# The second-last output block of a conv + maxout-FFN kernel: stored by SyncE in two halves instead of by GpSimd as a whole

## The chip, the core and the metric

The kernel runs on one core of one Trainium2 chip. The metric is the device time of one execution in microseconds (us). The profile of one execution is read beside it: its span runs from the first to the last instruction that the profiler recorded on the core, and the execution's own time is a little longer than that span.

Five engines matter, each with its own instruction stream: TensorE (PE), VectorE (DVE), ScalarE (ACT), GpSimd (POOL) and SyncE (SP). SP only issues DMAs and waits. DMAs are issued here from SP, ACT and POOL, and show in the profile as queue q1 (SP), q10 (ACT) and q0 (POOL).

## The reference

```python
# attention stage: softmax over 7 taps per head, then a causal 7-tap convolution along the sequence
w = exp(weight - max); w = w / (sum(w) + 1e-09)              # weight: 8 heads x 7 taps
x_pad = zeros(6 rows) + x                                    # x: 8 x 4160 x 192
out[b, s, h*24+g] = sum_k w[h, k] * x_pad[b, s + k, h*24+g]
# FFN stage on the 33280 tokens of 192
h = maximum(maximum(x @ w1, x @ w2), x @ w3)                 # 192 -> 768
y = h @ w_out                                                # 768 -> 192, float32
```

The output is 33280 rows of 192 float32 numbers, 768 bytes a row.

## The kernel before, in words

The tokens are cut into 65 blocks of 512 (`NBLK`). Blocks 0 to 63 are eight blocks from each of the eight sequences. Block 64 gathers the last 64 rows (`HALF`) of each sequence. The order of all instructions is written out by hand (`tc.manual_schedule()`), so what stands first in the text is issued first on its engine.

The main loop runs `t` from 1 to 64. Each turn does the following.

- It computes the first FFN layer of block `t` in six pieces `l1(t, j)`, j from 0 to 5: TensorE fills two PSUM tiles, `lp` and `lq` (L383), ScalarE makes `r` from `lp` (L387), VectorE makes `h` from `r` and `lq` (L388).
- Between these pieces it computes the second layer of the block before, `st2(t - 1, j, NJ)`, also in six pieces. TensorE accumulates into PSUM tiles `po` (L426). When two of a block's four 128-token slices are ready, ScalarE copies one partial sum to `a` (L435) and VectorE adds the other and writes the output tile `o` (L436). This happens at j = 3 for the first two slices and at j = 5 for the last two.
- It convolves a later block (`conv`), repacks it by DMA (`repack`, L366, half on SP and half on POOL; `double`, L372, on SP) and loads x for a later block (`load_x`, L130, on SP). These stop as the loop runs out of blocks.
- At the end of the turn, `store(t - 1, 0, 4, (nc.gpsimd,))` issues one DMA on POOL that writes the whole 512 x 192 tile `o` of block `t - 1` (L452).

After the loop, `st2(64, u, 6)` finishes block 64. Its four slices end one by one, and after each pair there are two stores of 64 partitions x 2 slices x 192: for slices 0 and 1 both on SP, for slices 2 and 3 one on SP and one on ACT. So the kernel ends with five stores: block 63 from POOL (393 KB) and block 64 from SP, SP, SP and ACT (98 KB each).

```python
if t == NB - 1 and s % 2 == 1:
    store(t, s - 1, s + 1, (nc.sync, nc.sync if s == 1 else nc.scalar))
```

Behind the last of these instructions stands the closing code of the program, which the profile shows under L542. SP waits for every DMA counter of the program, a few counters to each instruction. Every engine runs a DRAIN and reports to POOL. POOL, after a DRAIN of its own, waits for the four reports and then releases the others. A second round of the same kind follows.

Of the kernel before, what the change touches and what calls it, by code (L numbers as in the profile page):

```python
# [27 lines left out]
def kernel(  # L28
# [12 lines left out]
    nc = tc.nc  # L41
# [27 lines left out]
    NB = len(blocks)  # L69
# [41 lines left out]
    def load_x(t):  # L111
        if not 0 <= t < NB:
            return
        chunks = chunks_of[t]
        n = len(chunks)
        xf = (xfp.tile([P, NQ, D], FP32, tag="xf", name=f"xf_{t}") if n <= NQ else
              const.tile([P, n, D], FP32, name=f"xf_{t}"))
        parts = []
        i, n = 0, len(chunks)
        row = [c[1] * SEQ + c[2] for c in chunks]  # L120
        while i < n:
            k = i
            while (k + 1 < n and chunks[k + 1][3] == chunks[i][3]
                   and row[k + 1] - row[k] == row[i + 1] - row[i]):
                k += 1
            step = row[i + 1] - row[i] if k > i else 0
            rlen = chunks[i][3]
            src = bass.AP(tensor=x.tensor, offset=row[i] * D,
                          ap=[[D, rlen], [step * D, k - i + 1], [1, D]])
            nc.sync.dma_start(out=xf[0:rlen, i:k + 1, :], in_=src)  # L130
            if parts and parts[-1][0] == rlen:
                parts[-1] = (rlen, parts[-1][1], k + 1)
            else:
                parts.append((rlen, i, k + 1))
            i = k + 1
        xin[t] = [xf, None, parts]

    def cast_x(t):
        if not 0 <= t < NB:
            return  # L140
        xf, _, parts = xin[t]
        n = len(chunks_of[t])
        x16 = x16s[t % 4] if n <= NQ else x16z
        v = x16[:, EDGE:EDGE + n * D].rearrange("p (q d) -> p q d", d=D)
        for (rl, q0, q1) in parts:
            nc.gpsimd.tensor_copy(out=v[0:rl, q0:q1, :], in_=xf[0:rl, q0:q1, :])  # L146
        xin[t][1] = x16
# [164 lines left out]
    def conv(t, pools=((psw, "w"), (psw, "w"))):  # L312
        if t >= NB:
            return
        G = [pool.tile([P, NBLK], FP32, tag=tag, name=f"G{i}_{t}") for i, (pool, tag) in enumerate(pools)]
        x16 = xin[t][1]
        for (q, b, row_lo, rlen, lo, hi, cc) in chunks_of[t]:
            for i in range(2):
                for g in range(4):
                    h = SLOTS[i][g]  # L320
                    cb = q * D + GRP * h + EDGE * (g % 2)
                    nc.tensor.matmul(  # L322
                        G[i][32 * g:32 * g + 32, lo:hi],
                        lhsT=x16[0:rlen, cb:cb + 32],
                        rhs=band[0:rlen, h, cc:cc + hi - lo],
                        start=True, stop=True, tile_position=(0, 32 * g))
        slots[t] = ysp.tile([P, 2, NBLK], FP16, tag="ys", name=f"ys_{t}")
        convs[t] = G
        xin.pop(t)
# [20 lines left out]
    def evac(t, i, copy=nc.scalar.copy):  # L350
        if t >= NB:
            return
        copy(out=slots[t][:, i, :], in_=convs[t][i][:])  # L353
# [5 lines left out]
    def repack(t):  # L359


        if t >= NB:
            return
        yd = dense[t] = ydp.tile([P, NC, NBLK], FP16, tag="yd", name=f"yd_{t}")
        for n, (half, s0, c, r0, rows) in enumerate(pieces):
            (nc.sync, nc.gpsimd)[n % 2].dma_start(out=yd[r0:r0 + rows, c, :],  # L366
                                                  in_=slots[t][s0:s0 + rows, half, :])

    def double(t):

        if NDENSE <= t < NB:
            nc.sync.dma_start(out=dense[t][HALF:P, :, :], in_=dense[t][0:HALF, :, :])  # L372

    def l1(t, j):


        N, y = blkN[t], dense[t]
        ps = [pool.tile([P, NBLK], FP32, tag=tag, name=f"l{tag}_{t}_{j}")
              for pool, tag in ((psp, "p"), (psq, "q"))]
        for c in range(NC):  # L380
            for i in range(2):
                row = slice(HALF * i, HALF * (i + 1))
                nc.tensor.matmul(ps[i][:, 0:N], lhsT=wd[row, c, P * j:P * (j + 1)],  # L383
                                 rhs=y[row, c, 0:N],
                                 start=(c == 0), stop=(c == NC - 1))
        r = rp.tile([P, NBLK], FP16, tag="r", name=f"r_{t}_{j}")
        nc.scalar.activation(out=r[:, 0:N], in_=ps[0][:, 0:N], func=AF.Relu)  # L387
        nc.vector.tensor_max(out=hs[t][:, j, 0:N], in0=r[:, 0:N], in1=ps[1][:, 0:N])  # L388
# [52 lines left out]
    def store(t, s0, s1, qs):  # L441
        if t < 0:
            return
        ob, segs = outs[t], blocks[t]
        if len(segs) == 1:
            r = segs[0][0] * SEQ + segs[0][1] + P * s0
            todo = [(0, P, r, P)]
        else:
            assert all((b, S, n, off) == (b, SEQ - HALF, HALF, HALF * b) for b, S, n, off in segs)
            todo = [(HALF * i, HALF, (2 * s0 + i) * SEQ + SEQ - HALF, 2 * SEQ) for i in range(2)]  # L450
        for i, (p0, n, r, step) in enumerate(todo):
            qs[i].dma_start(out=bass.AP(tensor=out.tensor, offset=r * D,  # L452
                                        ap=[[D, n], [step * D, s1 - s0], [1, D]]),
                            in_=ob[p0:p0 + n, s0:s1, :])

    assert all(n == NBLK for n in blkN)
    def begin(t):
        hs[t] = hp.tile([P, NJ, NBLK], FP16, tag="h", name=f"h_{t}")
        outs[t] = outp.tile([P, 4, D], FP32, tag="o", name=f"o_{t}")
# [33 lines left out]
    for t in range(1, NB):  # L493
        u = t + AHEAD
        load_x(t + 7)
        cast_x(t + 5)
        double(u - 1)
        begin(t)
        l1(t, 0)
        if t == 1:  # L500
            conv(u)
            evac(u, 0)
            evac(u, 1)
        elif t % 2 == 0:
            conv(u)
            conv(u + 1, ((psp, "p"), (psq, "q")))
            evac(u, 0)
            evac(u + 1, 0)
            evac(u + 1, 1, nc.vector.tensor_copy)
            evac(u, 1, nc.vector.tensor_copy)  # L510
        repack(u)
        st2(t - 1, 0, NJ)
        for j in range(1, NJ):
            l1(t, j)
            st2(t - 1, j, NJ)
        store(t - 1, 0, 4, (nc.gpsimd,))
    for u in range(NJ):
        st2(NB - 1, u, NJ)
# [28 lines left out]
```

The softmax here doesn't subtract the row's maximum and nothing guards it: scores larger than these inputs give would overflow.

## Time and profile before

| | |
|---|---|
| median of 5 runs | 482.11 us (481.77 to 484.03) |
| the profiled execution's own time | 481.93 us |
| its span | 479.9 us |
| mean granted TensorE clock | 0.995 |
| TensorE (PE) busy | 467.7 us, 97% of the span |
| VectorE, ScalarE, GpSimd busy | 365.9, 327.1, 211.2 us |
| last matmul group of the timeline starts | 473.04 us |
| last compute instruction (VectorE, tile `o`) | 474.08 to 474.43 us |

The profiled execution's time is 2.0 us longer than its span. Times in the views are counted from the start of the span. Register, branch, semaphore and DMA-issuing instructions are not counted as busy, and the chain of waits follows computing engines, so the closing code shows only when its line is asked for. A "q" behind an engine's name (SPq, POOLq) marks its sequencer.

### The profile page before, as it was taken

The numbers are of one execution on the slowest core, as the hardware profiler recorded it, in microseconds if no ns is written. First come the engines' busy times: TensorE is split into PE (matmuls) and PEld (weight loads), VectorE is DVE, ScalarE is ACT, GpSimd is POOL, SyncE is SP. The second block draws the span as 40 slices with busy tenths as digits, with TensorE's granted clock in tenths as the row PEclk, the third lists the DMA queues.
The fourth block names the chain that finished last, engine by engine and source line by source line (L and its number), as shares of the span: only waits on it lengthen the run. The fifth ranks groups of instructions, "written<-read, shape, count | busy, mean of one in ns | idle before, by whom it ended". The sixth has DMA issues, their size and how long they took to land.

```text
span 479.9 us, 21944 instructions
## 1 busy us (share of the span) xinstructions
PE 467.7 (97%) x9083; PEld 393.9 (82%) x9083; DVE 365.9 (76%) x609; ACT 327.1 (68%) x608; POOL 211.2 (44%) x341
## 2 busy tenths in 40 slices
PE   7899999999999999999999999999999999999994
PEld 3578888888888888888888888888888888888994
DVE  6667778777777878777787777778777777778774
ACT  5676676676667667676766766676676767667663
POOL 2654543554354355435435543543545354345210
PEclk9899999999999999999999999999999999999999
DMA  8877747665666666566566566665556666544312
GB/s 194 223 192 210 217 137 201 180 180 159 194 183 182 172 184 172 168 175 190 164 178 191 157 166 193 169 190 172 163 170 182 193 172 177 163 137 135 113 44 95
DMA packets 67603, 82.08 MB, mean 171 GB/s; under 512 B 9424, under 2 KB 55760, under 8 KB 67504
## 3 DMA queue, kind: packets, MB, share of 16 engines
q1 hardware_dynamic: 53934, 49.01, 40.0%
q0 software_dynamic: 13216, 31.38, 18.6%
q8 instruction: 71, 1.16, 1.1%
q10 hardware_dynamic: 354, 0.30, 0.2%
q14 instruction: 28, 0.23, 0.2%
HBM read 30.31 MB, written 25.56 MB: 116 GB/s over the span
## 4 chain that ended last, share of the span: by engine, by line
PE 97%; DVE 1%; ACT 1%; issue 0%; POOL 0%; POOLq 0%
PE lp L383 32%; PE po L426 30%; PE lq L383 26%; PE G L322 7%; PE D L342 1%; PE idle L196 1%; ACT band L268 0%; PE band_sum L245 0%; ACT r L387 0%; DVE xz L216 0%; DVE h L388 0%; PE pm L305 0%; PE wps L223 0%; PE pm L301 0%; DVE band L218 0%
## 5 line engine op out<-in xcount | busy, mean ns | idle before, releaser
L388 DVE TENSOR_TENSOR h<-r,lq 128x512 f16<-128x512 f16 x390 | 267.0, 685 | 101.8 <-ACT r L387 101.8
L387 ACT ACTIVATE r<-lp 128x512 f16<-128x512 f32 x390 | 232.8, 597 | 135.2 <-PE lp L383 89.8
L383 PE MATMUL lp<-yd,wd 64*128 64x512 f16 x1170 | 315.0, 376 | 0.1
L383 PE MATMUL lq<-yd,wd 64*128 64x512 f16 x1170 | 314.4, 375 | 0.0
L426 PE MATMUL po<-wo,h 64*128 64x192 f16 x3120 | 231.4, 243 | 0.5 <-issue 0.5
L426 PEld LDWEIGHTS <-h 64*128 64x128 f16 x3120 | 187.0, 94 | 26.4 <-issue 0.7
L383 PEld LDWEIGHTS <-wd 64*128 64x128 f16 x2340 | 164.6, 93 | 20.4 <-issue 0.7
L452 POOL DMA_DIRECT2D out_dram<-o x64 | 50.7, 792 | 246.0 <-DVE o L436 234.0
L366 POOL DMA_DIRECT2D yd<-ys x189 | 95.5, 509 | 2.3 <-ACT ys L353 1.6
L426 PE MATMUL po<-m,yd 64*128 64x192 f16 x780 | 87.0, 243 | 0.0
L436 DVE TENSOR_TENSOR o<-a,po 128x384 f32<-128x384 f32 (+1 forms) x132 | 71.4, 541 | 0.6 <-ACT a L435 0.6
L146 POOL CAST x<-xf 112x960 f16<-112x960 f32 x62 | 61.6, 995 | 2.9 <-DMA xf<-in_x_dram 1.7
L435 ACT COPY a<-po 128x384 f32<-128x384 f32 (+1 forms) x132 | 61.8, 469 | 1.2 <-PE po L426 1.2
L426 PEld LDWEIGHTS <-yd 64*128 64x128 f16 x780 | 55.1, 94 | 8.1
L322 PEld LDWEIGHTS <-x 112*32 112x32 f16 x2480 | 29.7, 96 | 13.3 <-issue 13.2
L353 DVE CAST ys<-G 128x512 f16<-128x512 f32 x60 | 38.5, 682 | 0.1
L353 ACT CAST ys<-G 128x512 f16<-128x512 f32 x66 | 35.8, 589 | 2.0 <-PE G L322 0.7
L322 PE MATMUL G<-band,x 112*32 112x103 f16 (+1 forms) x2480 | 34.7, 209 | 0.0
L161 POOL CAST xz<-xf 112x240 f16<-112x240 f32 (+2 forms) x6 | 2.4, 448 | 10.5 <-DMA xf<-in_x_dram 10.5
L196 PE MATMUL idle<-idle 128*128 128x512 f16 x14 | 5.6, 539 | 1.2 <-DVE unit L212 1.2
L342 PE MATMUL D<-band,xz 112*32 112x103 f16 (+1 forms) x240 | 4.3, 249 | 1.1 <-ACT band L268 1.1
L342 PEld LDWEIGHTS <-xz 112*32 112x32 f16 x240 | 4.0, 120 | 1.6 <-issue 1.5
(50 smaller groups left out, 40.9 us busy)
## 6 DMA issues: line engine op xcount, KB each, us to landing
out_dram<-o POOLq DMA_DIRECT2D x64, 384.0 KB, 4.1
xf<-in_x_dram SPq DMA_DIRECT2D x57, 420.0 KB, 4.6
yd<-yd SPq DMA_DIRECT2D x63, 192.0 KB, 3.3
yd<-ys SPq DMA_DIRECT2D x63, 48.0 KB, 3.7
yd<-ys POOLq DMA_DIRECT2D x63, 48.0 KB, 3.3
xf<-in_x_dram SPq DMA_DIRECT2D x8, 252.0 KB, 3.0
yd<-ys SPq DMA_DIRECT2D x63, 32.0 KB, 3.3
yd<-ys POOLq DMA_DIRECT2D x63, 32.0 KB, 3.1
```

What stands on the lines that cost most here:

```text
L146: nc.gpsimd.tensor_copy(out=v[0:rl, q0:q1, :], in_=xf[0:rl, q0:q1, :])
L322: nc.tensor.matmul(G[i][32 * g:32 * g + 32, lo:hi], lhsT=x16[0:rlen, cb:cb + 32], rhs=band[0:rlen, h, cc:cc + hi - lo], start=True, stop=T ...
L342: nc.tensor.matmul(ps[32 * g:32 * g + 32, lo:hi], lhsT=xz[t][0:rlen, q, v, 32 * s:32 * s + 32], rhs=band[0:rlen, h, cc:cc + hi - lo], star ...
L353: copy(out=slots[t][:, i, :], in_=convs[t][i][:])
L366: (nc.sync, nc.gpsimd)[n % 2].dma_start(out=yd[r0:r0 + rows, c, :], in_=slots[t][s0:s0 + rows, half, :])
L383: nc.tensor.matmul(ps[i][:, 0:N], lhsT=wd[row, c, P * j:P * (j + 1)], rhs=y[row, c, 0:N], start=(c == 0), stop=(c == NC - 1))
L387: nc.scalar.activation(out=r[:, 0:N], in_=ps[0][:, 0:N], func=AF.Relu)
L388: nc.vector.tensor_max(out=hs[t][:, j, 0:N], in0=r[:, 0:N], in1=ps[1][:, 0:N])
L426: nc.tensor.matmul(ps[b0, i][:, s % 2, :], lhsT=a, rhs=b, start=first, stop=last)
L435: nc.scalar.copy(out=a[:, ss, :], in_=ps[s0, 0][:, ss, :])
L436: nc.vector.tensor_add(out=outs[t][:, s0:s + 1, :], in0=a[:, ss, :], in1=ps[s0, 1][:, ss, :])
L452: qs[i].dma_start(out=bass.AP(tensor=out.tensor, offset=r * D, ap=[[D, n], [step * D, s1 - s0], [1, D]]), in_=ob[p0:p0 + n, s0:s1, :])
```

## The change

The loop's last turn (t = 64) no longer stores block 63 from POOL as a whole. Directly after j = 3, when slices 0 and 1 of block 63 have been added up, SP is given a store of these two slices (128 partitions x 2 x 192, 196 KB). At the end of the turn SP is given the store of slices 2 and 3. All other blocks are stored as before.

```diff
         for j in range(1, NJ):
             l1(t, j)
             st2(t - 1, j, NJ)
-        store(t - 1, 0, 4, (nc.gpsimd,))
+            if t == NB - 1 and j == 3:
+                store(t - 1, 0, 2, (nc.sync,))
+        if t == NB - 1:
+            store(t - 1, 2, 4, (nc.sync,))
+        else:
+            store(t - 1, 0, 4, (nc.gpsimd,))
     for u in range(NJ):
         st2(NB - 1, u, NJ)
```

In the built program SP's stream ends with five stores in place of three: block 63's two halves, then block 64's three. POOL's stream ends with the store of block 62. The streams of TensorE, VectorE and ScalarE are the same.

## The prediction

> **What bounds the kernel now.** I read the page first, then the chain of waits, then the timeline of the last 10 us, and last the closing code's line, L542, engine by engine. The chain is TensorE nearly everywhere, and it stops early:
>
> ```profile
> PE 97%; DVE 1%; ACT 1%; issue 0%; POOL 0%; POOLq 0%
> ```
>
> ```profile
> 473.75 0.32 ACT a L435
> 474.06 0.02 issue
> 474.08 0.35 DVE o L436
> ```
>
> The last computing instruction ends at 474.43, the span at 479.9. So 5.5 us pass after it, with stores and closing code only. The change touches nothing else: on TensorE, VectorE and ScalarE the instruction streams are the same, and up to 469 us the program is unchanged. What must be known is which wait ends last in these 5.5 us. The timeline gives the stores (columns: start, length, engine):
>
> ```profile
> 471.98 0.55 DVE L436 TENSOR_TENSOR o<-a,po 128x384 f32<-128x384 f32 x1
> ...
> 472.76 0.62 DVE L436 TENSOR_TENSOR o<-a,po 128x192 f32<-128x192 f32 x2 [0.23 <-ACT a L435]
> ...
> 472.83 0.75 POOL L452 DMA_DIRECT2D out_dram<-o  x1 [5.61 <-DVE o L436]
> ...
> 473.41 2.06 SPq L452 DMA_DIRECT2D out_dram<-o  x3
> ...
> 474.47 0.65 ACTq L452 DMA_DIRECT2D out_dram<-o  x1
> ```
>
> Then the closing code, SP's (475.5 to 478) and POOL's (up to 479.15), and for comparison POOL's first drain of the program, under L531:
>
> ```profile
> L542 SPq EVENT_SEMAPHORE  x9: 17/28/28, 475.5 to 477.8; - x9
> L542 SPq DRAIN  x2: 7/7/7, 477.8 to 477.9; - x2
> ```
>
> ```profile
> L542 POOLq DRAIN  x1: 6327/6327/6327, 472.8 to 472.8; - x1
> ```
>
> ```profile
> L531 POOLq DRAIN  x1: 183/183/183, 0.3 to 0.3; - x1
> ```
>
> SP has seen the last store land and has reported at 477.91 (the record's own start, 477.908, plus 7 ns). POOL's drain, which starts as its last store is issued, lasts 6.327 us and ends at 472.805 + 6.327 = 479.13. POOL's next instruction, the wait for the four reports, starts at 479.18 and waits for nothing; from there to the end of the span are 0.735 us. So the end is set by POOL's drain, and SP has 1.26 us to spare. The drains of POOL with no DMA before them took 0.18 us (above), 0.10 and 0.04 us (the two at 479.3 and 479.6). The long one is the only one that follows a POOL store, so I put its length down to that store.
>
> The Trainium skill, "Perfetto Trace Analysis", section "Sequencer-only Instruction (DRAIN, etc)", says that the profiled stretch of such an instruction begins when its waits are met, so that the 6.3 us would be work or flushing on POOL itself, not a wait for another engine. The record alone does not show that.
>
> **The change, part by part.**
>
> POOL's store goes. POOL's last DMA becomes block 62's, issued at 466.47. Its drain then starts at about 466.45. With the same 6.33 us it ends at 472.8, over 5 us before SP reports; if it is as short as the other drains, sooner still. Either way SP's report is what ends last. Its start 477.908 + 0.007, plus 0.044 us from the last report to POOL's next instruction (at the program's start POOL's drain ends at 0.496 and the next record starts at 0.540), gives 477.96 in place of 479.18: **1.22 us less**, if SP reports as early as before.
>
> SP's closing list gets shorter behind the last landing. SP checks the DMA counters in a fixed order, one instruction about 0.06 us after the other (nine records end the list: eight from 477.355 to 477.784, then the drain). Before, the last store's counter was the first in the list, so all the others came after the landing, seven waits. In the changed program the stores take the counters in turn, and the last one has the third: five waits are left behind it. 2 x 0.06 = **0.12 us less**.
>
> The first half moves to SP at j = 3. It waits for the VectorE add of 468.80 to 469.35. SP has nothing between 451.6 and 473.4, so nobody queues behind that wait but its own later stores. Issue costs 0.6 to 0.7 us (the three stores on SP: 596, 627 and 694 ns), landing 2.4 to 2.6 us after the start, all before 472.2. The engines move nothing then. Cost: nothing; the empty stretch of 4 us hides it.
>
> The second half on SP waits for the add that ends at 472.53 and is issued at about 472.57. At 0.69 us it leaves SP free at 473.31 with the 0.05 us gap that its issues have. Block 64's first store needs the add of 473.38 and started at 473.41. So **nothing is delayed as long as this issue takes at most 0.79 us**. Behind it stand all three SP stores of block 64, and the closing list waits for them. SP's issues of this kernel:
>
> ```profile
> L366 SPq DMA_DIRECT2D yd<-ys x189: 513/588/2417, 22.5 to 447.7; - x189
> L130 SPq DMA_DIRECT2D xf<-in_x_dram x73: 317/584/3772, 0.7 to 416.8; - x73
> ```
>
> The medians (588 and 584 ns, the second with up to 560 rows of 768 bytes against the half's 256) say that the length does not follow the number of rows; the long ones stand mostly where much other traffic runs. I take 0.65 us, zero delay; the far end is 2.42 us, a delay of 1.63 us, to be kept for the rivals.
>
> The transfers at the end change shape:
>
> ```profile
> q1 hardware_dynamic: 432, 0.30, 37.0%
> q0 software_dynamic: 69, 0.20, 18.9%
> q10 hardware_dynamic: 144, 0.10, 13.7%
> ```
>
> (474.6 to 477.3: queue, packets, MB, share.) Before, POOL's 393 KB ran alone from 474.16 to 475.10 at about 430 GB/s. Block 64's first row started only at 475.11, although its issue had ended at 474.11; where nothing is in the way, rows of an SP issue start 0.65 us after its end (the 2 x 112 load at 0.74: 0.648; the doublings, median 0.666), which is 474.76. So POOL's store held block 64 back by 0.35 us. From 475.11 on, 576 packets took 1.88 us; the third SP store, issued until 475.48 and able to start at 476.13, still had ScalarE's rows beside it and posted its last packet at 476.99. One store alone needs 0.5 us (144 packets, first to last of the first one: 475.11 to 475.62). After: the second half's rows start at 472.57 + 0.65 + 0.65 = 473.87, and 272 packets at the pace of 144 in 0.5 us take 0.95 us, until 474.82. The first store of block 64 starts there in place of 475.11, 0.3 us earlier, and the others follow in line; the third cannot start before 476.13 and not end before 476.63. So the last landing is **0.2 to 0.36 us earlier; I take 0.25**. If the half's own first row comes as late as block 64's did (1.70 us after the issue started), it ends at 475.2 and nothing is won: lower bound zero, or 0.1 us lost.
>
> Sum: 1.22 + 0.12 + 0.25 = 1.59 us. The profiled execution (481.93, span 479.9) would take 480.3; the median of the runs lies 0.2 us above it, so the forecast is 482.11 - 1.6 = **480.5 us**. The parts' ends give a gain of 1.24 (all certain parts, 0.1 lost in the transfers) to 1.70 us, 480.4 to 480.9.
>
> A rule of the skill speaks against this: "DMA: Bandwidth & Descriptors", section "Rules for kernel authors", with "Issuing engines are not separate DMA queues", says that all issuers share the same 16 DMA engines, that spreading DMAs over them saves only issue time, and that one large transfer beats two. By it the change would be worth nothing, since SP pays one issue more than POOL saves: 482.1. The row of the drain speaks otherwise, because it prices POOL as issuer and not the transfer.
>
> **The rivals.**
>
> *POOL's drain ends with the traffic, not with its own store.* There is one long drain in the trace, so a tie to the last landing cannot be excluded: it ended 1.78 us after 477.355. For it: the store itself had landed 2.9 us after its issue, at 475.7, so the drain outlived it by 3.4 us, which I cannot explain. Against it: the drain carries no wait. Then only the transfers' 0 to 0.36 us are won: 481.75 to 482.2. Chance 0.11.
>
> *SP becomes the bound, and later than POOL was.* One issue of the second half of d us delays block 64's three SP stores by d - 0.79. The gain of 1.59 is eaten at d = 2.4, just the longest issue in the steady part (2.417: even), and beyond that it is slower: at 3.77 us, the longest at all, 2.98 - 1.59 = 1.4 us slower, 483.5. For it: one code load per 8 to 9 us runs on the DMA engines, and the one at 471.61 to 472.48 ends just before. Against it: the medians, and no backlog before this issue. Chance 0.06.
>
> *The change is real but smaller*, a delay of 0.3 to 1 us from a slower issue or packets that queue: 480.8 to 481.5. Chance 0.08, and it lies on both sides of the bound below.
>
> **How the numbers follow.** About 0.3%, 1.45 us, is what a measurement of this kernel can tell from no change, and the forecast's gain stands close to it. The forecast has 0.75; its interval of 1.24 to 1.70 lies above 1.45 for the values I hold likelier, four fifths of it: 0.60 faster, 0.15 within. The first rival goes within 0.3%: 0.11. The third: 0.02 faster, 0.06 within. The slower rival: 0.04 slower, 0.02 within; the median of five runs that reach up to 484.03 adds some scatter, for which I move 0.02 more from "within" to slower. Sums: 0.62, 0.32, 0.06. The range from 479.9 to 481.7 holds the forecast with the runs' scatter of 0.3 to 0.5 us, the third case, and leaves out most of the first rival and the slower one.
>
> **What would show it.** Right: POOL's drain starts at about 466.5 and is over long before 477; SP's drain at 477.4 to 477.8 is directly followed by POOL's wait for the reports; the last DMA packet is at 476.6 to 477.0; block 64's first SP store still starts at 473.41. Wrong: a POOL drain that still ends behind SP's report, a second-half issue longer than 0.8 us, or a last packet after 477.1.

## The result, and the profile after

Over 43 runs the changed kernel takes 481.3 us (median), the kernel before 482.85 us over 80 runs. The ratio is 0.9971, 95% interval 0.9960 to 0.9982: 1.4 us faster, between 0.9 and 1.9. The time forecast, 480.5 us, lies 0.8 us below the measured one, mostly because it was counted from the 482.11 us of five runs; over 80 runs the kernel before takes 0.74 us more. So what can be compared is the gain: 1.6 us forecast, 1.4 measured.

The profiled execution of the changed kernel is not one to set beside the old one as a whole: 482.97 us, span 481.2 us, longer than before. Its last matmul starts at 476.26 us, not at 473.46, and this difference arises between 21 and 25 us, where the two programs are the same. The waits of that stretch (19 to 27 us) show it: engine, what waited, what for, total, times, longest.

```profile
PE pm L301 <- issue: 3.2, 1, 3.2
```

TensorE stood there for 3.2 us for no reason that the profile shows; in the old execution the same wait took 0.2 us. In the twelve profiled executions of kernels whose POOL issues DMAs, the last matmul starts between 473.3 and 477.6 us, so much of the runs' scatter arises ahead of the end; in which stretch was looked up for this execution alone. What the change does must be read behind them, so from here on I use the **tail**: from the start of the last matmul to the end of the span. It is 6.45 us before (479.91 - 473.46) and 4.90 us after (481.16 - 476.26): **1.55 us less**. Executions of both kernels that were profiled again gave 6.46 and 4.92.

POOL's drain and SP's closing list in the changed kernel (the closing code is now line L547; first POOL up to 480.4 us, then SP from 478.2 to 480.5, then POOL behind that):

```profile
L547 POOLq DRAIN  x1: 6245/6245/6245, 469.2 to 469.2; - x1
```

```profile
L547 SPq EVENT_SEMAPHORE  x9: 17/28/28, 478.3 to 480.3; - x9
L547 SPq DRAIN  x2: 7/10/13, 480.3 to 480.4; - x2
```

```profile
L547 POOLq EVENT_SEMAPHORE  x4: 17/17/17, 480.4 to 481.1; - x4
L547 POOLq DRAIN  x2: 40/71/102, 480.6 to 480.9; - x2
```

The drain is as long as it was, but it runs from 469.25 to 475.49, while TensorE is still computing. SP's second drain, its report, starts at 480.396 and POOL's wait for the reports passes at 480.429, right behind it. Before, POOL came 1.26 us after SP. The end is now SP's.

The stores, from the timeline (start, length, engine) and by line:

```profile
474.79 0.55 DVE L436 TENSOR_TENSOR o<-a,po 128x384 f32<-128x384 f32 x1
...
475.36 2.87 SPq L452 DMA_DIRECT2D out_dram<-o  x4
...
477.28 0.66 ACTq L452 DMA_DIRECT2D out_dram<-o  x1
```

```profile
L452 SPq DMA_DIRECT2D out_dram<-o x5: 396/606/703, 472.2 to 477.6; - x5
...
DMA to landing us min/median/max: 1.9/2.0/2.3
```

The second half is issued 0.03 us after its add and takes 0.396 us. SP is free at 475.76, and block 64's first store starts at 476.22, as far from the last matmul (-0.05 us) as before. Nothing is delayed.

### The profile page after: what moved, and what is told of

Read it like the earlier page. It is cut to its first block, busy times and chain, and to the rows that moved or that the text cites. A ratio compares the mean times of both kernels' runs of the same rounds, so it can differ in the third digit from the quotient of the medians.

```text
span 481.2 us, 21943 instructions
## 1 busy us (share of the span) xinstructions
PE 467.6 (97%) x9083; PEld 392.6 (82%) x9083; DVE 366.0 (76%) x609; ACT 327.2 (68%) x608; POOL 210.4 (44%) x340
## 4 chain that ended last, share of the span: by engine, by line
PE 94%; DMA 4%; issue 1%; POOL 0%; ACTq 0%; SPq 0%; DVE 0%; ACT 0%
PE lp L383 32%; PE po L426 30%; PE lq L383 26%; PE G L322 7%; DMA xf<-in_x_dram 2%; DMA ws<-in_moe_w_dram 1%; PE pm L301 0%; POOL x L146 0%; PE pm L305 0%; ACTq L176 0%; SPq L186 0%; DVE o L436 0%; ACT a L435 0%
## 5 line engine op out<-in xcount | busy, mean ns | idle before, releaser
L254 DVE TENSOR_TENSOR wd<-ws,w3s 128x384 f16<-128x384 f32 (+1 forms) x4 | 3.1, 778 | 1.7 <-issue 1.2
L301 PE MATMUL pm<-wo,w3t 128*128 128x192 f16 x6 | 1.1, 363 | 3.2 <-issue 3.2
```

## The experiments

Tails in one table, all times in us from the start of the last matmul of the same execution. "POOL's last" is the end of POOL's last instruction ahead of its drain; "drain" is how long after that the drain ended.

| kernel | POOL's last ends | drain | drain ends | SP reports | tail |
|---|---|---|---|---|---|
| before | 0.12 | 5.55 | 5.67 | 4.46 | 6.45 |
| changed | -6.24 | 5.47 | -0.77 | 4.14 | 4.90 |
| second half on POOL | 0.07 | 5.56 | 5.63 | 4.21 | 6.41 |
| first half on POOL | -3.11 | 6.11 | 3.01 | 4.20 | 4.96 |
| whole on SP | -6.24 | 5.47 | -0.77 | 4.20 | 4.96 |
| late POOL copy | 1.23 | 5.49 | 6.72 | 4.30 | 7.51 |
| late copy, no POOL DMA | 1.23 | 0.07 | 1.30 | 4.06 | 4.75 |
| counter sixth | -6.24 | 5.47 | -0.77 | 3.97 | 4.73 |
| counter last | -12.59 | 5.39 | -7.20 | 4.27 | 5.03 |
| counter eighth | -6.24 | 5.47 | -0.77 | 4.53 | 5.29 |
| half in two of 64 | -6.24 | 5.47 | -0.77 | 4.62 | 5.38 |
| before, once more | 0.12 | 5.55 | 5.68 | 4.44 | 6.46 |
| changed, once more | -6.24 | 5.47 | -0.77 | 4.16 | 4.92 |

Each row is one execution. In every row the tail is the later of "drain ends" and "SP reports" plus 0.76 to 0.78 us (0.69 in the row without POOL DMAs, where POOL's later drain and clear are shorter too).

**Second half back on POOL.** This tells the issuing engine from the halving.

```diff
         if t == NB - 1:
-            store(t - 1, 2, 4, (nc.sync,))
+            store(t - 1, 2, 4, (nc.gpsimd,))
```

> Block 63's first half on SP after j = 3 as in the changed kernel, its second half on POOL. Tail = from the start of the last matmul to the end of the span (before 6.45 us, changed kernel 4.90 us). My theory: POOL's drain is priced by POOL's own last store. It starts with that store's issue, 0.6 us ahead of the last matmul's start, lasts 6.2 to 6.3 us although the store is half as large, and ends the kernel again: tail 6.3 to 6.45 us, ratio to before 1.000 (0.999 to 1.001). Rival, the gain came from halving the store and from fewer late bytes on POOL: tail 5.2 to 5.8 us, ratio 0.998 or less. Rival, the drain ends with the traffic: it would end 1.8 us behind the last landing, and as the landing comes 0.2 us earlier, tail 6.2 us.

Ratio to before 1.0008 (0.9976 to 1.0040); tail 6.41 us. POOL's closing line up to 481 us:

```profile
L547 POOLq DRAIN  x1: 6283/6283/6283, 474.6 to 474.6; - x1
L547 POOLq EVENT_SEMAPHORE  x1: 17/17/17, 480.9 to 480.9; - x1
```

Half the bytes, an earlier last landing (3.71 against 3.90 us) and nearly the same end. The halving alone is worth 0.04 us at most. A drain tied to the last landing would have ended 0.2 us earlier, one tied to the landing of POOL's own store 0.58 us earlier (1.65 against 2.23 us); it ended 0.04 us earlier, by as much as POOL's issue was shorter (707 against 752 ns).

**The whole block on SP.** This takes away the early half.

```diff
-            if t == NB - 1 and j == 3:
-                store(t - 1, 0, 2, (nc.sync,))
-        if t == NB - 1:
-            store(t - 1, 2, 4, (nc.sync,))
-        else:
-            store(t - 1, 0, 4, (nc.gpsimd,))
+        store(t - 1, 0, 4, (nc.sync if t == NB - 1 else nc.gpsimd,))
```

> Block 63 stored on SP as a whole at the end of the turn, no first half. My theory: the drain is out of the way as in the changed kernel, and what the early half is worth is the transfer time of 256 rows, 0.6 us, of which a part is hidden behind block 64's issues: tail 4.9 to 5.4 us, last packet 0 to 0.5 us later than in the changed kernel, ratio to before 0.997 to 0.998. Rival, the two halves matter and not the issuing engine: tail 6 us or more, ratio 0.999 to 1.000.

Ratio 0.9941 (0.9911 to 0.9971); tail 4.96 us, last packet at 3.33 us as in the changed kernel (3.32). The 512 rows of 768 bytes were through at 1.26 us; block 64's first row came at 1.31, as in the changed kernel (1.32). So the split saves no transfer time that anyone waits for; the 0.06 us come from the last store's counter, which stands one place further ahead in SP's list (second, not third). The ratio lies lower than the changed kernel's, but the intervals overlap, and the tails say that the two are the same.

**One late instruction on POOL.** This asks what the drain's 5.5 us hang on.

```diff
     for u in range(NJ):
         st2(NB - 1, u, NJ)
+    late = const.tile([P, 1], FP32)
+    nc.gpsimd.tensor_copy(out=late[:], in_=outs[NB - 1][:, 3, 0:1])
```

> The changed kernel with one more instruction on POOL: a copy of one column of block 64's output tile, which waits for the last vector add, 1.0 us after the start of the last matmul. It leaves POOL's last store 7 us back. Theory A, the drain waits for something that ends 6.3 us after the last POOL store, by the clock: the drain after the copy takes 0.2 us or less, tail 4.9 us, ratio to before 0.997. Theory B, the first drain behind any POOL stores costs 6.2 us of work from its own start: it ends 7.2 us after the last matmul's start, tail 8.0 us, ratio to before 1.003. I hold A a little likelier.

Ratio 1.0057 (1.0027 to 1.0087); tail 7.51 us. POOL's copy and its drain:

```profile
L525 POOL COPY late<-o x1: 189/189/189, 475.2 to 475.2; 128x1 f32<-128x1 f32 x1
```

```profile
L549 POOLq DRAIN  x1: 5700/5700/5700, 475.2 to 475.2; - x1
```

Theory A, which I held a little likelier, fell. The last store was 7 us old, and still the drain ended 5.49 us after the 0.19 us copy. Theory B was right in kind and 0.5 us too long (7.2 us forecast for the drain's end, 6.72 measured): its 6.2 us still held the issue of a store, 0.75 us, where here stands a copy of 0.19. The tail grew by 2.6 us over the changed kernel for one column copied. By its ratio this kernel is 2.7 us slower than before, between 1.3 and 4.2; the tail accounts for 1.05 of it. Where the rest lies is open: the profiled execution, at 483.75 us the fastest of its 12 runs, does not show it. Two of the 12 runs, 483.75 and 483.83 us, lie where the tail alone would put them; the other ten take 485.6 to 488.7 us, and none of them was profiled.

**The same copy, without any DMA from POOL.** Repacking and all stores go through SP.

```diff
-            (nc.sync, nc.gpsimd)[n % 2].dma_start(out=yd[r0:r0 + rows, c, :],
+            nc.sync.dma_start(out=yd[r0:r0 + rows, c, :],
...
-            store(t - 1, 0, 4, (nc.gpsimd,))
+            store(t - 1, 0, 4, (nc.sync,))
```

> The late POOL copy again, but no DMA of the whole kernel is issued from POOL: repacking and all stores are on SP. The total time may change for that; only the tail is read. Theory A, the 5.5 us drain is the price of having issued DMAs on POOL, however long ago: the drain takes 0.2 us or less and SP's report ends last, tail 4.9 to 5.2 us. Theory B, the first drain behind POOL's work takes 5.5 us whether or not POOL issued DMAs: tail 7.5 us as in the run with the copy and POOL's DMAs.

The kernel as a whole takes 490.07 us in its one run. Its tail is 4.75 us:

```profile
L549 POOLq DRAIN  x1: 276/276/276, 484.5 to 484.5; - x1
```

The same drain behind the same copy is over 0.07 us after it. So the 5.5 us are the price of DMAs that POOL issued earlier, due at POOL's first drain behind them, and counted from the end of whatever POOL does last. What POOL does in these 5.5 us the traces do not show. How old the DMAs may be is not shown either: the oldest last DMA in these runs was issued 8 us ahead of the copy, and no run kept the repacking on POOL, whose last DMA is 25 us old there, with all stores on SP.

**First half on POOL.** POOL may still store, if it is early enough.

```diff
             if t == NB - 1 and j == 3:
-                store(t - 1, 0, 2, (nc.sync,))
+                store(t - 1, 0, 2, (nc.gpsimd,))
```

> The changed kernel with the first half of block 63 on POOL after j = 3 instead of on SP. POOL's last DMA then ends 3.4 us before the last matmul starts (as of now its drain has taken 5.4 to 5.55 us from the end of POOL's last instruction in every run). Theory: the drain ends 2.2 us after the last matmul's start, 1.9 us ahead of SP's report, and nothing moves: tail 4.9 us, ratio to before 0.996 to 0.998. Rival, any store of block 63 on POOL costs the gain: tail 6.4 us, ratio 1.000.

Ratio 0.9977 (0.9955 to 0.9999); tail 4.96 us. POOL's drain and, behind it, the landing of POOL's store:

```profile
L547 POOLq DRAIN  x1: 6840/6840/6840, 472.6 to 472.6; - x1
```

```profile
DMA to landing us min/median/max: 4.0/4.0/4.0
```

As expected, the gain stays. The drain, expected to end at 2.2 us, took 6.11 us from the end of POOL's last instruction, the longest seen, and ended at 3.01 us, still 1.2 us ahead of SP's report. In the same execution POOL's store landed 4.0 us after its start, in place of 2.3 for the same shape in the run with the second half on POOL: its last three packets of data started between -1.09 and -0.39 us, 0.8 us and more behind the others, and a code load (one packet of 16 KB, kind "instruction") ran on the DMA engines from -2.43 to -1.09. So a store that is still moving may lengthen the drain; one execution does not show that it did.

**Second half in two stores of 64 partitions.** This gives SP one issue more ahead of block 64, with the same bytes.

```diff
-            store(t - 1, 2, 4, (nc.sync,))
+            r = (blocks[t - 1][0][0] * SEQ + blocks[t - 1][0][1] + 2 * P) * D
+            for p0 in (0, HALF):
+                nc.sync.dma_start(out=bass.AP(tensor=out.tensor, offset=r + p0 * D,
+                                              ap=[[D, HALF], [P * D, 2], [1, D]]),
+                                  in_=outs[t - 1][p0:p0 + HALF, 2:4, :])
```

> The changed kernel with the second half of block 63 in two stores of 64 partitions on SP, each taking 0.6 to 0.7 us to issue in place of one of 0.40. SP is then free 0.4 to 0.5 us after it was, and block 64's first store, which had 0.05 us to spare ahead of its data, starts 0.4 to 0.5 us later. Theory, SP's row of issues sets the end now: last packet and tail later by the same: 5.3 to 5.4 us. Rival, the transfers have slack: tail 4.9 to 5.0 us.

The timeline of SP's issues, 470 to 480 us (last matmul at 475.14):

```profile
471.06 0.42 SPq L452 DMA_DIRECT2D out_dram<-o  x1
474.24 1.36 SPq L521 DMA_DIRECT2D out_dram<-o  x2
475.70 2.04 SPq L452 DMA_DIRECT2D out_dram<-o  x3
```

Block 64's first store starts at 0.56 us in place of -0.05, the third at 1.85 in place of 1.37. The last packet comes at 3.85 (3.32 before the split) and the tail is 5.38 us: 0.49 us for the third store, 0.53 for the last packet, 0.48 for the tail, since the last store's counter stands one place (0.06 us) further back in SP's list. So SP's row of issues sets the end now. Of the first store's delay of 0.61 us, 0.11 were made up because its issue took 0.60 us here and 0.70 in the changed kernel. SP came free 0.97 us later (at 0.46 in place of -0.51 us): what it had to spare ahead of block 64's data in the changed kernel was 0.4 us, not the 0.05 of the expectation.

**The last store's counter further back in SP's list.** Three kernels put more small stores into SP's idle time, so that the counters, dealt in turn, fall differently.

```diff
# counter sixth: first half in four stores (2 slices x 2 column halves)
-                store(t - 1, 0, 2, (nc.sync,))
+                r = (blocks[t - 1][0][0] * SEQ + blocks[t - 1][0][1]) * D
+                for s in range(2):
+                    for c in (0, D // 2):
+                        nc.sync.dma_start(out=bass.AP(tensor=out.tensor, offset=r + P * s * D + c,
+                                                      ap=[[D, P], [1, D // 2]]),
+                                          in_=outs[t - 1][:, s, c:c + D // 2])
# counter last: first half in two, and block 62 in four stores of one slice on SP
# counter eighth: first half in six (2 slices x 3 column thirds)
```

> The changed kernel with five more SP stores ahead of the end, in SP's idle time: block 62 goes to SP in four stores of one slice, block 63's first half in two. The DMA counters are dealt in turn, so the last store's counter is now the last of the eight in SP's closing list, not the third. My theory: five waits of 0.06 us fewer lie behind the last landing, and nothing else moves: tail 4.90 - 0.30 = 4.6 us, ratio to before 0.9965. Rival, each wait costs 0.06 us of looking whether or not its counter is met, and the list is hidden or reordered: tail 4.9 us. POOL's drain starts 6 us earlier and must not matter.

> The changed kernel with its first half in four stores of 128 partitions x 96 columns on SP, three stores more than before, in SP's idle time. The last store's counter moves from the third to the sixth place of SP's closing list. Theory: three waits of 0.06 us fewer behind the last landing, from there to SP's report 0.25 us in place of 0.43; tail 4.7 us, if the 0.3 us that SP lost between its two closing drains in the run with the counter last does not come back; 5.0 us if it does, and then it belongs to SP's longer instruction stream (that run had seven instructions more than the changed kernel, this one has four).

> The changed kernel with its first half in six stores of 128 partitions x 64 columns on SP: five stores more, so the last store's counter stands eighth and last in SP's closing list; SP's stream has seven instructions more than in the changed kernel, as many as in the run with block 62 on SP. Theory of the list: 0.30 us less from the last landing to SP's report, tail 4.60 us, ratio to before 0.996 to 0.997. If the 0.36 us gap between SP's two closing drains comes back, it belongs to the length of SP's stream, and the tail is 4.95 to 5.05 us; if not, it was an accident of the one profiled execution.

With the counter sixth the tail is 4.73 us: from the wait that the last landing ends (3.71 us) to SP's report 0.25 us in place of 0.43, as expected. With the counter last (ratio 0.9942, 0.9915 to 0.9968) the wait for the landing ends at 3.71 us and the first drain follows 0.08 us later, 0.29 us sooner behind it than in the changed kernel; then the gain is lost between the two drains, and the tail forecast at 4.6 us is 5.03. SP's closing line with the counter last and, for comparison, with it sixth:

```profile
L551 SPq EVENT_SEMAPHORE  x9: 17/28/28, 477.8 to 479.4; - x9
L551 SPq DRAIN  x2: 7/61/115, 479.5 to 479.9; - x2
```

```profile
L552 SPq EVENT_SEMAPHORE  x9: 17/28/28, 476.6 to 478.4; - x9
L552 SPq DRAIN  x2: 7/10/13, 478.5 to 478.5; - x2
```

The second drain starts 0.36 us after the first, in place of 0.06, and takes 115 ns: tail 5.03 us. With the counter eighth (ratio 0.9969, 0.9945 to 0.9992) the gap came back, 0.34 us and 130 ns. Both programs have seven instructions more in SP's stream than the changed kernel; the one with four more has no gap. That does not make the length the cause: in the same two programs the last store's counter stands last in the list, and SP's stream in the kernel without POOL DMAs, over 300 instructions longer, has no gap (SP's drains at 487.4 and 487.5 us):

```profile
L549 SPq DRAIN  x2: 7/10/13, 487.4 to 487.5; - x2
```

What SP waits for in the gap was not shown. The kernel with the counter eighth has a second loss that I had not expected. One of its six stores took 1.39 us to issue, in place of 0.39 to 0.43:

```profile
L520 SPq DMA_DIRECT2D out_dram<-o x6: 392/431/1387, 472.6 to 475.9; - x6
```

That took SP past the add of the second half, which was issued at -0.32 us in place of -0.90, and block 64's first store came 0.26 us late. The long issue (-2.22 to -0.84 us) runs beside a code load (-2.30 to -1.19 us); that the load is its cause was not shown. The tail is 5.29 us.

**Both kernels once more.**

> The changed kernel once more, for the scatter of its tail and for a ratio on one chip with the run that has the counter last: tail 4.85 to 4.97 us, ratio to before 0.996 to 0.998.

> The kernel before once more, for the scatter of its tail: 6.40 to 6.50 us, with POOL's drain ending 5.4 to 5.6 us behind the end of its last store's issue.

Tails 4.92 and 6.46 us; the changed kernel's ratio in this set was 0.9962 (0.9939 to 0.9985).

The kernel with the counter sixth beats both in the tail, by 0.17 us over the changed one. That is 0.04% of the time, below what the runs can tell apart, and the kernel with the counter sixth was run once only.

## Why the prediction was right, step by step

*What ends last.* Right. POOL's drain set the end, and behind the change it is SP's report. The step was worth 1.22 us in the sum; measured 1.235 (5.717 us to POOL's wait before, against SP's report at 4.456 plus 0.026).

*What the drain hangs on.* Here the step failed in its reason, though not in its number. I put the drain's length down to the store ahead of it. The copy without a store nearby drains for as long; without any POOL DMA it takes 0.07 us. That the number held was luck in part: it held because moving the store also removed POOL's last instruction. By my reason, a harmless-looking late copy would have been free; it costs 2.6 us. The Trainium skill's statement that such a record starts when its waits are met ("Perfetto Trace Analysis", "Sequencer-only Instruction (DRAIN, etc)") fits these runs: the drain carries no wait, and it takes 5.39 to 5.56 us from the end of POOL's last instruction in eleven of twelve executions, whatever traffic is under way. It starts 0.02 us ahead of that instruction, so its stretch holds POOL's own work too.

*The closing list.* 0.12 us forecast, 0.12 measured (0.553 to 0.432 us from the wait that the landing ends to SP's report); the run with the counter sixth shows the same 0.06 us per place.

*The second half's issue.* Taken at 0.65, measured 0.396 us. The room of 0.79 us was not used up. The 0.65 came from stores of 64 partitions; the store of 128 partitions, with twice the rows, takes less. The first half, taken at 0.6 to 0.7 us and 2.4 to 2.6 us to its landing, measured 0.42 and 1.97 us.

*The transfers.* 0.25 us forecast, 0.20 measured (landing 3.90 to 3.70 us), but by another way. I had the second half's rows run until 1.36 us after the last matmul's start; they were through at 0.69.

```profile
q1 hardware_dynamic: 272, 0.20, 23.3%
```

(Changed kernel, 474.5 to 477 us: 272 packets of the half; they run from 0.01 to 0.69 us, at about 350 GB/s in the middle.) Block 64's first row came at 1.32 us (1.65 before), which is where its own issue lets it start. From there the three issues of SP set much of the pace, as the run with two stores of 64 shows. They do not set all of it: the third is issued until 1.97 us, but its first row comes 0.91 us later, not 0.65, with ScalarE's rows still running (2.45 to 3.06 us), and its last packet at 3.32. So the store on POOL did hold block 64 back by 0.33 us, and 0.2 of it reached the end. The run with the counter sixth bears that out: its third store is issued until 2.02 us, as before, and its last packet comes at 3.33 in place of 3.53. The prediction lets POOL's 393 KB run alone until 475.10 us; 379 KB were through by then, the rest ran beside block 64's first rows until 475.33.

The sum: 1.235 + 0.12 + 0.20 = 1.55 us against 1.59. The runs' 1.4 us (0.9 to 1.9) agree.

*The rivals.* The drain that ends with the traffic is out (second half on POOL, late copy; in the changed kernel it is over before the last five stores land). SP is the bound now, as the main line said, and 1.55 us earlier than POOL was; the long issue that would have made it later did not come here. That the gain is smaller, 0.6 to 1.3 us, the runs alone cannot exclude (0.9 to 1.9); the tails, 1.5 us apart in two pairs of executions, speak against it. The skill's rule that spreading DMAs over issuers saves only issue time ("DMA: Bandwidth & Descriptors", "Issuing engines are not separate DMA queues") holds nearly for the transfers here: block 63's second half, issued from POOL or from SP, left the last landing at 3.71 and 3.70 us, and the whole block moved from POOL to SP brought it from 3.90 to 3.70, where the issue of 0.75 us became one of 0.42. It does not cover what an issuer owes at the end of the program.

*The bound of 0.3%.* The gain measured, 0.29%, lies on it, and its interval, 0.18 to 0.40%, on both sides, so the runs cannot say on which side it is.

## What to carry to other kernels

At the end of a kernel look at the closing code engine by engine, since the chain of waits does not show it: which engine's report comes last, and by how much. Where GpSimd has issued DMAs, give it nothing, neither a store nor a small copy, in the 6 us or so before the other engines report, if its drain is seen to take that long. Then the end belongs to the engine that issues the last stores, and here the number of its issues counted more than their bytes: the whole block in one late store cost no transfer time, the half in two stores 0.5 us.

## What the hardware showed that I had not expected

- POOL's first drain behind POOL-issued DMAs ended 5.4 to 6.1 us after POOL's last instruction in all twelve profiled executions of kernels with such DMAs, whether that was a store of 393 KB, one of 196 KB or a copy of one column 7 us after the last store. Without POOL DMAs: 0.07 us, in one execution.
- A store of 128 partitions x 2 x 192 takes SP 0.37 to 0.43 us to issue and its 272 packets 0.65 to 0.7 us; one of 64 partitions, with half the bytes, takes 0.60 to 0.75 us to issue and 0.45 to 0.8 us to move, beside the rows of other stores.
- Between the starts of SP's two closing drains lie 0.06 us in most programs and 0.34 to 0.36 us in the two whose last store has the last counter of SP's list and whose SP stream is seven instructions longer; which of the two it goes with is open.
